# Gateloop attention with a maxout FFN on one core: a new order of all engine lists, a new order of the last output parts, and three unread steps left out of the last group

## The chip, the core and the metric

The kernel runs on one core of a Trainium2 chip. The metric is the device time of one execution in microseconds; a kernel is run several times and the median counts. Beside these runs, one execution is taken with the hardware profiler. Its trace gives the times of every instruction, counted from the start of its span, on TensorE (PE, with its weight loads shown apart as PEld), VectorE (DVE), ScalarE (ACT), GpSimd (POOL) and SyncE (SP, which here only starts DMAs).

## What is computed

All is float32: 4 batches, 8 heads, 768 time steps, head size 48. The first half is a scan with a complex gate, the second a feed-forward layer on its result.

```python
mag = np.sqrt(a_re * a_re + a_im * a_im)
scale = np.minimum(mag, 0.999) / (mag + 1e-06)
a_re_n, a_im_n = (a_re * scale, a_im * scale)
for t in range(S):                       # 768 steps, state D x D per head
    new_re = ar * S_re - ai * S_im
    new_im = ar * S_im + ai * S_re
    kv = np.einsum('bhd,bhe->bhde', k[:, :, t], v[:, :, t])
    S_re, S_im = (new_re + kv, new_im)
    y[:, :, t] = np.einsum('bhd,bhde->bhe', q[:, :, t], S_re)
# x: y as (3072 tokens, 384 features); w1, w2, w3: 384 x 768; w_out: 768 x 384
h = np.maximum(np.maximum(x @ w1, x @ w2), x @ w3)
return h @ w_out
```

## The kernel before

**Groups.** The 768 time steps are cut into 12 groups of 64 (`NG`). In a group, the four batches are two pairs: pair x and pair y, each with its 64 steps of two batches on 128 partitions. A step of the program has a name, the pair where it has one, and its group: `dkx:3` is step `dk` of pair x in group 3.

**The steps of a group.** Loads (`Lr`, `Li` for the gate, `Lk`, `Lq`, `Lv`). The gate's logarithm and angle (`sqr`, `sqi`, `add`, `lnL`, ... `atan`, `turn`), on ACT and DVE. Running sums over time are matmuls with constant matrices: `cs` sums the angles (it needs `turn`), `sums` the logarithms (it needs `Lnop`), `F` makes sums for eighths of a group. `sums` has two halves, one with the matrix `mid` and one with the matrix `rest`. From `mid` come the factors `Ek` and `Eq` on keys and queries, from `rest` comes `En`. Keys and queries are multiplied by cosine and sine (`sa`, `sb`, then `uk`, `uq` on DVE), transposed on PE (`tpk`, `tpq`), copied out of PSUM (`Kc`, `Qc`) and scaled for blocks of time (`Q1`, `Q2`, `QB`, `QG`, `KB` on DVE). `A` and `B` are scores on PE; `g0` to `g3` (DVE) and `b0`, `b1` (ACT) bring them into the lower triangle. For the state that the next group reads, DVE multiplies the keys by `En` (`kEn`), PE multiplies them with the values (`dk`), and `h0` and `h1` add this to the state. `y` is the group's output on PE, from scores, values and state, and `x` copies it to SBUF. The last group has no `dk`.

**The feed-forward part.** In each group after the first, `U01`, `U11`, `U02`, `U12` are the big products with the up weights: 18 matmuls of 128x256 each in the trace. `u01` and `u11` (a maximum with zero) and `u02`, `u12` (a maximum on DVE) read them; the weights `w2` and `w3` are stored as differences from `w1`, whose share reaches the output by the product of `w1` and `w_out`, so two weights in two halves are all that `U` multiplies. The down product is cut into seven block products `P1` to `P7`, with sums of blocks `S1` to `S4` on DVE and two more products `Px`, `Py`. `P1`, `P6` share one half of a PSUM tile, `P5`, `P7` the other; in a second tile `P2`, `P3` write one half, and `P4` writes columns 0 to 191 of the other half, while `Py` has written all its columns. `r1` (ACT), `r6`, `r5`, `r7`, `r57`, `ox`, `oy` and, in the last group, `oz` (all DVE) add the products up into two output tiles, and `Dx`, `Dy`, `Dz` send them out, one DMA from SP's queue and, in the last group, one from ACT's queue. In the last group `oy` and `Dy` have columns 0 to 191 of pair y's output, `oz` and `Dz` columns 192 to 383.

**The first group.** Before group 0 ends, the weights have to be loaded and turned into the form that PE reads. Steps `WL`, `Wa`, `Wb`, `Wc`, `We`, `Wf`, `Wg` do that for twelve parts of the weights, in ACT and DVE between the steps of groups 0 to 2. `T`, `t`, `M`, `m` make the product of `w1` and `w_out` (transposes, their copy on ACT, matmuls, a copy on ACT).

**What sets the order.** The string `SCHEDULE` (lines 21 to 114) lists every step once. `program` runs through it, and each step issues its instructions. `Bound` (line 189) ties each instruction of an engine behind the one before it on that engine, so the list is also the order in which each engine works, and each DMA queue starts. Nothing else moves a step: an engine whose next step has to wait holds all steps behind it. `SLOTS` has a digit for every PSUM tile in the order in which they are asked for: one of four slots of two banks; a tile has to wait until the readers of the tile before it in that slot are done (`banks`, line 208). `OTHER` names the steps that run on their other engine: a copy or an absolute value on DVE in place of ACT, a load started by POOL in place of SP, an addition on DVE in place of a DMA that adds (started by POOL).

All instructions are issued from line 198, so views of the trace are read by tile: `sums<-Ln,rest` is the `rest` half of `sums`, `E<-sums` is `Ek` or `Eq`, `uk<-uk,En` is `kEn`, `cs<-w,upto` is `cs`, `w<-w,ar` is `turn`, `g<-dk` and `g<-g,dk` are `h1`, `vb<-wt` is `t0` or `t1`, `wm<-wo,vb` is `M0` or `M1`, `wm<-wo,uk` is `M2`, `up<-xhx,w` is one of the big products `U`, `op<-...` is one of `P1` to `P7`, `Px`, `Py`, and `ot<-ot,op` is one of `r6` to `oz`.

Of the kernel before, what the change touches and what calls it, by code (L numbers as in the profile page):

```python
# [21 lines left out]
Lix:0 sqi0:0 Zf:0 Zg:0 Lrx:0 xor0:0 sqr0:0 Liy:0 Lry:0 sqi1:0 add0:0 lnL0:0 expe0:0 expw0:0 xor1:0 lne0:0 relu0:0  # L22
Lnop0:0 WL0:0 sqr1:0 Wa0:0 add1:0 CL:0 lnL1:0 expe1:0 Lkx:0 abs0:0 Lix:1 Wb0:0 Wc0:0 We0:0 WL3:0 half0:0 expw1:0 Fx:0
lne1:0 relu1:0 Lnop1:0 pw0:0 Wa3:0 Wf0:0 abs1:0 Wb3:0 half1:0 WL6:0 lnw0:0 expL0:0 f3x:0 Liy:1 f2x:0 Lrx:1 Wc3:0 Wa6:0
f1x:0 Lry:1 mulai0:0 mulw0:0 We3:0 Wb6:0 WL9:0 pw1:0 lnw1:0 stt0:0 expL1:0 mulw1:0 f0x:0 atan0:0 mulai1:0 Wf3:0 T0:0
sqi:1 stt1:0 turn0:0 Wc6:0 atan1:0 Lqy:0 sumsx:0 csx:0 turn1:0 We6:0 Lqx:0 sqr:1 add:1 Wf6:0 Wa9:0 Wb9:0 WL11:0 WL10:0
# [10 lines left out]
b0y:0 Lky:1 b1y:0 kEny:0 Wf7:0 sumsy:1 f3:1 yy:0 mulw:2 xy:0 sb:1 dky:0 u02x:0 stt:2 U02y:0 Lkx:1 h1y:0 Z4:0 mqx:1
atan:2 U11y:0 Lnop:2 Wb8:0 mkx:1 turn:2 sa:1 ukx:1 u11y:0 U01y:0 U12y:0 u01y:0 Eky:1 uqx:1 u02y:0 Eqy:1 cs:2 u12y:0
tpqx:1 Wc8:0 We8:0 mky:1 Eny:1 Lky:2 tpkx:1 Qcx:1 Wf8:0 t:2 Wg7:0 U21y:0 Wg8:0 U21x:0 nfy:2 nfx:2 Q1x:1 Lqx:2 mqy:1
Q2x:1 kEnx:1 uqy:1 u21y:0 U22y:0 u22y:0 u21x:0 af:2 Kcx:1 sumsx:2 F:2 Ax:1 g0x:1 g1x:1 g2x:1 Ekx:2 Enx:2 Eqx:2 Z2:0  # L40
Lvx:1 f1:2 f3:2 KBx:1 h0x:1 uky:1 tpqy:1 f2:2 Qcy:1 Q1y:1 g3x:1 Oy:0 Lvy:2 tpky:1 Q2y:1 mqx:2 Lvy:1 f0:2 Lkx:2 sa:2
sqi:3 oy:0 Lry:3 J3:0 QBx:1 dkx:1 Bx:1 sb:2 h1x:1 U12x:0 QBy:1 uqx:2 QGx:1 U22x:0 Kcy:1 KBy:1 Lrx:3 Lqy:2 u22x:0
u12x:0 Ay:1 b1x:1 g0y:1 g1y:1 g2y:1 g3y:1 b0x:1 mkx:2 sqr:3 tpqx:2 Qcx:2 By:1 yx:1 add:3 lnL:3 QBx:2 expe:3 b0y:1
sumsy:2 xx:1 Eqy:2 Eky:2 expw:3 relu:3 Q1x:2 b1y:1 QGy:1 abs:3 Ox:0 Q2x:2 Lix:4 ukx:2 ox:0 mky:2 mqy:2 Dy:0 uky:2 yy:1
addw:3 tpky:2 lne:3 kEny:1 tpkx:2 Liy:4 Lnop:3 xy:1 xor:3 half:3 Cdy:2 Kcy:2 U11:1 Cdx:2 J1:0 U01:1 Lqx:3 Lrx:4 uqy:2
lnw:3 Kcx:2 KBx:2 J2:0 expL:3 u11:1 Dx:0 Eny:2 mulw:3 mulai:3 stt:3 kEny:2 h0y:1 tpqy:2 atan:3 Lry:4 sqi:4 turn:3
Qcy:2 dky:1 h1y:1 kEnx:2 sumsx:3 u01:1 J4:0 cs:3 Eqx:3 mqx:3 Ax:2 h0y:2 Ekx:3 t:3 sqr:4 add:4 g0x:2 g1x:2 g2x:2 U12:1
Enx:3 Lrx:5 nfx:3 U02:1 lnL:4 expe:4 Q1y:2 nfy:3 expw:4 u12:1 S3:1 af:3 dky:2 g3x:2 relu:4 abs:4 addw:4 Q2y:2 F:3
u02:1 Bx:2 Ay:2 Lvx:2 sb:3 S1:1 f2:3 Lkx:3 h1y:2 f1:3 QGx:2 Lqy:3 P5:1 S2:1 P7:1 f0:3 QBy:2 g0y:2 KBy:2 g1y:2 f3:3
S4:1 lnw:4 g2y:2 P1:1 expL:4 h0x:2 P6:1 r1:1 b0x:2 b1x:2 g3y:2 r6:1 dkx:2 r5:1 r7:1 lne:4 Lry:5 sa:3 Lky:3 r57:1 h1x:2  # L50
sumsy:3 By:2 xor:4 mkx:3 b1y:2 b0y:2 Eny:3 half:4 Cdy:3 Liy:5 yx:2 xx:2 mulw:4 Eky:3 Eqy:3 Py:1 QGy:2 Px:1 P4:1 P3:1
yy:2 ukx:3 uqx:3 xy:2 oy:1 tpkx:3 tpqx:3 mky:3 h0x:3 mulai:4 Kcx:3 Lix:5 sqi:5 stt:4 Qcx:3 Lqx:4 Lky:4 P2:1 uky:3
Lnop:4 atan:4 U01:2 ox:1 u01:2 tpky:3 Lvy:3 QGx:3 Kcy:3 mqy:3 Cdx:3 uqy:3 tpqy:3 turn:4 sumsx:4 Qcy:3 Lrx:6 kEny:3
KBx:3 h0y:3 Lkx:4 Q2y:3 QBx:3 Ekx:4 Enx:4 Q1y:3 Eqx:4 cs:4 F:4 f1:4 mkx:4 t:4 sqr:5 U11:2 u11:2 Lqx:6 f3:4 Q2x:3 f2:4
Dy:1 nfx:4 Q1x:3 nfy:4 Ay:3 add:5 g0y:3 Ax:3 f0:4 g0x:3 g1y:3 g2y:3 af:4 mqx:4 xor:5 Bx:3 g3y:3 sb:4 KBy:3 U02:2 sa:4
g1x:3 U12:2 ukx:4 u02:2 S3:2 g2x:3 tpkx:4 g3x:3 Lvx:3 uqx:4 Lvy:4 lnL:5 expw:5 relu:5 Lqy:4 u12:2 expe:5 Kcx:4 tpqx:4
Qcx:4 dky:3 kEnx:3 dkx:3 S1:2 h1y:3 sumsy:4 S2:2 P5:2 h1x:3 Eqy:4 QBy:3 Dx:1 abs:5 Liy:6 addw:5 b0x:3 b1x:3 lne:5
Lnop:5 half:5 Eky:4 mky:4 Eny:4 mqy:4 Cdx:4 S4:2 Cdy:4 P1:2 P6:2 Py:2 P4:2 r1:2 yx:3 r6:2 r5:2 By:3 lnw:5 expL:5 b0y:3
mulw:5 uqy:4 h0x:4 b1y:3 mulai:5 QGy:3 Px:2 stt:5 atan:5 Lix:6 P3:2 Lry:6 xx:3 sqr:6 Liy:7 P7:2 r7:2 Lkx:5 uky:4 P2:2
tpqy:4 Lky:5 Qcy:4 r57:2 tpky:4 yy:3 sqi:6 ox:2 Lqx:5 kEnx:4 kEny:4 Lvx:4 dkx:4 oy:2 add:6 xy:3 Kcy:4 sumsy:5 turn:5  # L60
sumsx:5 h1x:4 QGx:4 Dy:2 Dx:2 Ekx:5 cs:5 Q1y:4 lnL:6 Lix:7 Eqx:5 U11:3 mkx:5 expw:6 Lvx:5 relu:6 KBx:4 Q2x:4 Enx:5
expe:6 lne:6 h0y:4 Q2y:4 mqx:5 Eky:5 U01:3 Lnop:6 abs:6 Q1x:4 u11:3 t:5 nfy:5 nfx:5 Eny:5 QBx:4 u01:3 Eqy:5 mky:5
xor:6 Ax:4 af:5 g0x:4 addw:6 sb:5 dky:4 h1y:4 sa:5 F:5 half:6 f3:5 uqx:5 g1x:4 g2x:4 lnw:6 expL:6 U12:3 u12:3 f2:5
Lrx:7 f0:5 f1:5 U02:3 tpqx:5 g3x:4 mulai:6 uky:5 tpky:5 Qcx:5 mulw:6 u02:3 Lqy:5 S1:3 Ay:4 Bx:4 S2:3 P1:3 QBy:4 sqi:7
S3:3 mqy:5 b1x:4 P5:3 Kcy:5 b0x:4 KBy:4 g0y:4 P6:3 stt:6 g1y:4 uqy:5 By:4 atan:6 yx:4 ukx:5 P7:3 g2y:4 g3y:4 Lkx:6
Lry:7 sqr:7 QGy:4 b0y:4 b1y:4 Cdy:5 Cdx:5 Q1x:5 tpkx:5 xx:4 Kcx:5 turn:6 tpqy:5 add:7 S4:3 Qcy:5 Lvx:6 r1:3 yy:4 xy:4
sumsx:6 Eqx:6 cs:6 t:6 lnL:7 r6:3 Px:3 kEnx:5 r5:3 Q2x:5 Py:3 P4:3 Enx:6 h0x:5 Ekx:6 xor:7 nfy:6 kEny:5 P2:3 U01:4
r7:3 nfx:6 expw:7 dkx:5 expe:7 lne:7 relu:7 abs:7 r57:3 addw:7 QGx:5 af:6 Lry:8 Lvy:5 h1x:5 mqx:6 sb:6 Lqy:6 u01:4
sumsy:6 QBx:5 sa:6 F:6 Liy:8 U11:4 f3:6 Eqy:6 mkx:6 Q2y:5 Eky:6 KBx:5 mqy:6 P3:3 Lky:6 Q1y:5 f1:6 uqy:6 Lrx:8 h0y:5
f0:6 oy:3 Eny:6 ox:3 Bx:5 u11:4 KBy:5 lnw:7 Ax:5 g0x:5 Ay:5 g1x:5 half:7 g2x:5 expL:7 f2:6 g3x:5 mulai:7 U02:4 g0y:5  # L70
g1y:5 g2y:5 b0x:5 g3y:5 QBy:5 b1x:5 mky:6 yx:5 ukx:6 By:5 Lvy:6 Dx:3 Cdy:6 u02:4 Cdx:6 QGy:5 mulw:7 b1y:5 uqx:6 U12:4
P1:4 S3:4 b0y:5 P7:4 stt:7 atan:7 Lqx:7 xx:5 u12:4 S1:4 tpqx:6 tpkx:6 S2:4 Kcx:6 yy:5 turn:7 Lnop:7 dky:5 Qcx:6 uky:6
Lkx:7 r1:4 sqr:8 sumsx:7 xy:5 h1y:5 cs:7 t:7 kEnx:6 Lix:8 sqi:8 P6:4 Px:4 Py:4 P5:4 P2:4 P4:4 QBx:6 Dy:3 h0x:6 add:8
lnL:8 relu:8 Q1x:6 expw:8 nfx:7 Q2x:6 Eqx:7 expe:8 S4:4 nfy:7 P3:4 tpqy:6 r6:4 KBx:6 Lqx:8 abs:8 Liy:9 r5:4 r7:4 Ekx:7
r57:4 tpky:6 ox:4 oy:4 Enx:7 af:7 dkx:6 Qcy:6 kEny:6 F:7 Dx:4 sa:7 xor:8 h1x:6 half:8 sb:7 h0y:6 Lkx:8 Dy:4 f0:7 f2:7
Q2y:6 f1:7 QGx:6 U11:5 u11:5 Cdx:7 mkx:7 U12:5 Kcy:6 u12:5 Q1y:6 Lry:9 Cdy:7 U01:5 Lrx:9 Lix:9 mqx:7 addw:8 f3:7 ukx:7
# [994 lines left out]
```

## Time and profile before

| | us |
|---|---|
| median of 3 runs | 551.74 |
| lowest and highest run | 549.87, 553.06 |
| the profiled execution, its own time | 552.02 |
| its span, first to last instruction | 550.3 |
| PE busy in the span | 515.6 (94%) |
| DVE busy | 484.8 (88%) |
| ACT busy | 363.8 (66%) |
| POOL busy | 115.6 (21%) |

A row of the table of windows has a stretch of the span, its length, then for PE, PEld, DVE, ACT and POOL the busy time in it with the number of instructions, then PEclk (the mean clock that PE was granted, 1.00 is full), the busy share of the DMA engines and GB/s. A row of waits has the engine and the tile that waited, the engine and tile that ended the wait, the total in us, the number of waits, and the longest. A row of the timeline has start, duration, engine, line, operation, tiles, forms and count, and in brackets the idle time of the engine ahead of it and what ended it; "issue" means that the engine waited for nothing that the profile shows. A row of the chain of work that ended last has start, duration, engine, tile and count. Queue q8 brings PE's instructions.

### The profile page before, as it was taken

The page shows a single profiled execution, that of the slowest core. Times are in us where ns is not written, and L with a number is a line of the kernel's source. Part 1 is how long each engine was busy: PE and PEld are TensorE (multiplying, and loading weights), DVE is VectorE, ACT ScalarE, POOL GpSimd, SP SyncE. Part 2 cuts the span into 40 slices and gives each one's busy share as a digit, 9 for nine tenths or more (in the row PEclk, how much of TensorE's full clock was granted, in tenths as well). Part 3 has the DMA queues.
Part 4 walks back from the last instruction along what each step waited for, and adds up shares of the span by engine and source line. Part 5 has one row for each costly group of instructions (what it writes and reads, how often), then busy time and mean ns, then how long its engine had stood idle before and what let it go on. Part 6 is the DMA issues. An engine that isn't in the chain of part 4 may idle for free.

```text
span 550.3 us, 22368 instructions
## 1 busy us (share of the span) xinstructions
PE 515.6 (94%) x9998; PEld 441.4 (80%) x9998; DVE 484.8 (88%) x735; ACT 363.8 (66%) x568; POOL 115.6 (21%) x167
## 2 busy tenths in 40 slices
PE   2478989999999999999999999999999899999996
PEld 1245578778988888988898988988988788988886
DVE  7999989999999999999999999988999687886325
ACT  6999898688989778696492638677678465221000
POOL 7524180030251222214004001303101250000000
PEclk9769899999999999999999999999999899999999
DMA  8978975553443455244516025356150350010011
GB/s 233 243 206 170 244 129 89 101 92 69 80 89 74 96 111 104 49 91 83 104 42 121 3 52 107 64 105 112 22 104 11 66 117 2 4 30 4 2 29 29
DMA packets 117023, 47.93 MB, mean 87 GB/s; under 512 B 103936, under 2 KB 109536, under 8 KB 116928
## 3 DMA queue, kind: packets, MB, share of 16 engines
q1 hardware_dynamic: 104272, 31.87, 27.4%
q0 software_dynamic: 10304, 14.05, 14.1%
q8 instruction: 78, 1.28, 0.9%
q10 hardware_dynamic: 2352, 0.59, 0.5%
q14 instruction: 17, 0.14, 0.1%
HBM read 33.03 MB, written 4.72 MB: 69 GB/s over the span
## 4 chain that ended last, share of the span: by engine, by line
PE 71%; DVE 10%; issue 2%; ACT 1%; DVEq 0%; ACTq 0%
PE up L198 28%; PE op L198 22%; PE y L198 6%; PE tp L198 4%; PE A L198 3%; PE dk L198 3%; PE sums L198 2%; DVE atm L198 1%; PE B L198 1%; DVE Q L198 1%; PE F L198 1%; DVE QG L198 1%; PE cs L198 1%; DVE uk L198 1%; DVE xhx L198 1%
## 5 line engine op out<-in xcount | busy, mean ns | idle before, releaser
L198 PE MATMUL up<-xhx,w 128*128 128x256 f32 x792 | 177.5, 382 | 0.0
L198 PEld LDWEIGHTS up<-xhx,w 128*128 128x128 f32 x792 | 148.6, 190 | 22.4 <-DVE g L198 2.2
L198 ACT ACT_TABLE_LOAD x50 | 64.2, 1283 | 4.4 <-issue 3.6
L198 POOL DMA_DIRECT2D ar<-nf x44 | 39.9, 1297 | 77.8 <-DVE ar L198 66.7
L198 ACT COPY atm<-B 32x128 f32<-32x128 f32 x96 | 24.5, 256 | 39.4 <-DVE atm L198 24.2
L198 PE MATMUL op<-wo,xhx 128*128 128x192 f32 (+1 forms) x220 | 49.2, 362 | 0.0
L198 DVE TENSOR_TENSOR Q<-Q,f 112x1024 f32<-112x1024 f32 (+1 forms) x48 | 45.3, 951 | 0.4 <-ACT Q L198 0.2
L198 PE MATMUL y<-atm,vb 128*32 128x64 f32 x1152 | 39.4, 221 | 2.9 <-issue 2.9
L198 PEld LDWEIGHTS op<-wo,xhx 128*128 128x128 f32 x220 | 36.7, 190 | 3.3 <-issue 0.6
L198 PEld LDWEIGHTS y<-atm,vb 128*32 128x32 f32 x1152 | 33.1, 110 | 7.3 <-issue 6.2
L198 PE MATMUL y<-QG,g 112*32 112x64 f32 x1408 | 37.3, 220 | 0.5 <-issue 0.5
L198 DVE TENSOR_TENSOR ot<-ot,op 128x192 f32<-128x192 f32 (+1 forms) x67 | 27.1, 413 | 11.0 <-PE op L198 6.2
L198 DVE TENSOR_TENSOR xhx<-xhx,up 128x768 f32<-128x768 f32 x22 | 20.9, 951 | 17.9 <-PE up L198 17.9
L198 PEld LDWEIGHTS y<-QG,g 112*32 112x32 f32 x1408 | 34.6, 110 | 0.7 <-issue 0.7
L198 PE MATMUL op<-wo,strassen 128*128 128x192 f32 x176 | 34.2, 339 | 0.1
L198 POOL DMA_DIRECT2D w<-L x8 | 9.0, 1124 | 117.4 <-ACT L L198 104.8
L198 PE MATMUL op<-w,strassen 128*128 128x192 f32 x176 | 32.8, 329 | 0.0
L198 DVE COPY_PREDICATED atm<-masko,A 128x256 f32<-128x256 uint8 x72 | 31.2, 435 | 1.2
L198 PEld LDWEIGHTS op<-wo,strassen 128*128 128x128 f32 x176 | 30.0, 196 | 2.3 <-issue 0.7
L198 PE MATMUL A<-Q,K 112*32 112x80 f32 x1536 | 30.6, 234 | 0.5 <-issue 0.5
L198 PEld LDWEIGHTS op<-w,strassen 128*128 128x128 f32 x176 | 28.9, 190 | 1.9 <-ACT ot L198 0.8
L198 PEld LDWEIGHTS A<-Q,K 112*32 112x32 f32 x1536 | 27.4, 110 | 3.6 <-issue 1.4
(156 smaller groups left out, 1114.5 us busy)
## 6 DMA issues: line engine op xcount, KB each, us to landing
ai<-in_a_im_dram SPq DMA_DIRECT2D x46, 96.0 KB, 3.4
ar<-in_a_re_dram SPq DMA_DIRECT2D x46, 96.0 KB, 3.3
out_dram<-ot SPq DMA_DIRECT2D x45, 96.0 KB, 3.0
...
```

The costliest lines, as they stand in the source:

```text
L198: ins = f(*a, **kw)
```

## The change

One line of code changes: in the last group `sums` leaves out its `rest` half.

```diff
         if name == "sums":
             ps = T["sums", x] = banks("sums")
-            for n, mat in enumerate((mid, rest)):
+            for n, mat in enumerate((mid, rest) if g < NG - 1 else (mid,)):
```

`SCHEDULE`, `SLOTS` and `OTHER` are replaced as a whole. The new list has the same 1752 steps less four: `Enx:11`, `Eny:11`, `kEnx:11`, `kEny:11`. Of `OTHER`, 32 names go and 37 come: loads of keys, queries and values change between the queues of SP and POOL in both directions; on DVE come `abs:3`, `abs:8`, `af:9`, `u01:8`, `u11:5`, `u11:7`, `Qcy:7`, `Kcx:11`, `Lnop:9` and `addw` of groups 6 to 11; from DVE go `abs:5`, `abs:6`, `af:5`, `af:7`, `af:8`, `u01:3`, `u01:11`, `u11:6`, `addw:5`, and copies `Kc`, `Qc` and `x` of groups 6 to 10, eight of them.

The places of the list that matter most, before and after. The stretch around `cs:1`:

```diff
-uqx:0 tpqx:0 lnw:1 t0:0 Wf11:0 WL1:0 T1:0 WL2:0 Wf10:0 expL:1 Qcx:0 Lky:0 ukx:0 tpkx:0 mulw:1 Wa1:0 t1:0 Cdx:0 Lvx:0
-Eqy:0 Kcx:0 Wa2:0 lne:1 Q2x:0 Fy:0 f2y:0 Wb1:0 f1y:0 WL4:0 kEnx:0 Q1x:0 M0:0 f3y:0 Liy:2 f0y:0 Eny:0 mulai:1 Wb2:0
...
-dkx:0 Lrx:2 Lry:2 sqr:2 add:2 atan:1 lnL:2 Wb4:0 Cdy:0 turn:1 WL5:0 Wg1:0 Wc4:0 M1:0 h1x:0 expe:2 cs:1 relu:2 g1x:0
+Wf1:0 Fy:0 f0y:0 We2:0 stt:1 Wf2:0 Ax:0 Lnop:1 Eky:0 Eqy:0 mqy:0 t0:0 f1y:0 f2y:0 WL4:0 WL5:0 mky:0 f3y:0 g0x:0 sby:0
+sqi:2 sqr:2 add:2 afy:0 dkx:0 h1x:0 M0:0 atan:1 Cdy:0 turn:1 Wa4:0 Wb4:0 M1:0 cs:1 Wg1:0 say:0 M2:0 lnL:2 g1x:0 Wc4:0
```

The stretch from `U12:8` to `yx:9`:

```diff
-KBy:9 Ax:9 g0y:9 lne:11 By:9 U12:8 expw:11 g1y:9 mkx:10 g0x:9 g1x:9 g2y:9 g3y:9 relu:11 P1:8 Lvx:9 b0y:9 abs:11 ukx:10
-g2x:9 g3x:9 S3:8 tpkx:10 u12:8 mqx:10 b1y:9 b1x:9 b0x:9 sumsy:10 F:10 Kcx:10 yx:9 S1:8 f3:10 f1:10 addw:11 Eqy:10 xx:9
+af:10 Ax:9 By:9 expe:11 g2y:9 mkx:10 Eqx:10 U12:8 sa:10 Dy:7 g0x:9 g1x:9 lne:11 expw:11 g3y:9 g2x:9 b0y:9 ukx:10 g3x:9
+b1x:9 tpkx:10 sumsy:10 Lnop:11 b0x:9 u12:8 b1y:9 Dx:7 Kcx:10 F:10 S1:8 f0:10 Lqy:10 f2:10 S3:8 yx:9 kEnx:10 h0x:9 P7:8
+S2:8 abs:11 Eny:10 f1:10 P6:8 P1:8 xor:11 half:11 Cdy:10 addw:11 Eqy:10 mqy:10 uqy:10 Cdx:10 f3:10 QGy:9 P5:8 S4:8
```

The end:

```diff
-u02:11 Dy:10 S3:11 P1:11 r1:11 P2:11 S1:11 S2:11 P5:11 S4:11 P6:11 kEny:11 P3:11 r6:11 r5:11 ox:11 P7:11 P4:11 r7:11
-r57:11 Dx:11 oy:11 Dy:11 oz:11 Dz:11
+P2:10 P3:10 r7:10 r57:10 U01:11 oy:10 Dy:10 u01:11 U02:11 U12:11 ox:10 Dx:10 Py:11 Px:11 u11:11 u12:11 P1:11 r1:11
+u02:11 P2:11 S3:11 S1:11 P5:11 S2:11 S4:11 P6:11 r6:11 P3:11 r5:11 P7:11 ox:11 P4:11 Dx:11 r7:11 r57:11 oz:11 Dz:11
+oy:11 Dy:11
```

More of the change, by code (lines that the diff above doesn't have):

```diff
@@ L21 @@
 SCHEDULE = """
[L22 to L26, printed above, removed]
@@ L37 @@
[L37 to L41, printed above, removed]
@@ L42 @@
[L42 to L76, printed above, removed]
@@ L87 @@
-Lix:11 atan:9 h0x:8 yy:7 Lqy:9 oy:6 tpky:8 xy:7 KBx:8 Cdy:8 Lvx:8 Kcy:8 tpqy:8 sumsy:9 Lkx:9 F:9 Qcy:8 f0:9 U11:7
-sqi:10 ox:6 f2:9 Eqy:9 kEny:8 Eky:9 Cdx:8 Dx:6 turn:9 Q1y:8 u11:7 Dy:6 U12:7 kEnx:8 xor:10 f1:9 dky:7 mqy:9 Eny:9
-sqr:10 add:10 dkx:8 f3:9 mky:9 u12:7 h1x:8 sumsx:9 Q1x:8 Lqx:9 Lry:11 cs:9 Q2y:8 S3:7 lnL:10 Lrx:11 t:9 Liy:11 QGx:8
-Eqx:9 h1y:7 nfx:9 Q2x:8 relu:10 h0y:8 expw:10 U01:7 expe:10 lne:10 abs:10 nfy:9 addw:10 u01:7 U02:7 Ekx:9 half:10
-u02:7 Bx:8 Ax:8 Ay:8 S1:7 sb:9 Enx:9 P5:7 af:9 QBy:8 g0x:8 sa:9 g1x:8 S2:7 g2x:8 g0y:8 P1:7 lnw:10 Lnop:10 KBy:8 g3x:8
@@ new lines @@
+Cdx:5 g0y:4 uqy:5 b1x:4 KBy:4 P5:3 QBy:4 b0x:4 g1y:4 g2y:4 P6:3 sqi:7 Kcy:5 atan:6 yx:4 Lqx:6 Lkx:6 Lry:7 sqr:7 kEny:5
+By:4 g3y:4 P7:3 ukx:5 b1y:4 tpqy:5 QGy:4 b0y:4 QBx:5 Dx:2 turn:6 r1:3 Lry:8 r6:3 tpkx:5 xx:4 r5:3 add:7 Kcx:5 yy:4
+Qcy:5 kEnx:5 xy:4 r7:3 sumsx:6 cs:6 Ekx:6 Q1y:5 xor:7 r57:3 Enx:6 Lqy:6 t:6 nfy:6 nfx:6 lnL:7 expe:7 Py:3 QGx:5 P4:3
+Px:3 af:6 S4:3 lne:7 Eqx:6 expw:7 h0y:5 KBx:5 h0x:5 Q2x:5 sa:6 Lix:8 mqx:6 U01:4 P2:3 u01:4 sb:6 sumsy:6 F:6 dkx:5
+P3:3 h1x:5 Q2y:5 f3:6 relu:7 Eny:6 abs:7 half:7 Eqy:6 mqy:6 f2:6 U11:4 addw:7 oy:3 f0:6 f1:6 ox:3 Ax:5 Lrx:8 mkx:6
@@ new lines @@
+sumsy:7 Lkx:8 Lvx:7 r7:5 r57:5 cs:8 dky:6 kEnx:7 Q1x:7 Lry:10 P3:5 Eky:7 mky:7 Eqy:7 h1y:6 t:8 nfy:8 P4:5 mqy:7 uqy:7
+xor:9 Eny:7 U01:6 expe:9 lne:9 KBx:7 QBx:7 u01:6 U11:6 nfx:8 oy:5 af:8 relu:9 u11:6 h0y:7 Q2x:7 QGx:7 ox:5 uky:7
+tpky:7 Kcy:7 Dy:5 tpqy:7 dkx:7 Qcy:7 sumsx:8 sumsy:8 Ax:7 h1x:7 Ekx:8 Eqx:8 mkx:8 Lqx:8 expw:9 abs:9 U12:6 Eny:8
+kEny:7 Q2y:7 Eqy:8 addw:9 g0x:7 Enx:8 mqx:8 Lvy:8 Q1y:7 g1x:7 g2x:7 g3x:7 U02:6 sa:8 F:8 sb:8 Eky:8 Lky:8 f1:8 u12:6
+uqx:8 tpqx:8 Qcx:8 ukx:8 f0:8 u02:6 S1:6 Bx:7 Lqy:8 Lnop:9 Ay:7 Lvx:8 b1x:7 S3:6 S2:6 g0y:7 half:9 P5:6 Dx:5 mky:8
@@ L119 @@
[L119 removed]
+0123102012312312032102130130103121020120320312303210310130201321032101230102103210321301302132132132
+0110231023131023012300321301102310123223021301302130230200132123102310213023213103203102310321021302
+1301230130120123021013203203121213021302310213023021312103
 """
 OTHER = set("""
[L123 to L124 removed]
```

120 lines of the change are left out of this document (78 added, 42 removed).

## The prediction, made before the change was run

> **What bounds the kernel now.** The page comes first, for its busy times; then the table of windows, cut where PE waited long; then the waits of PE; then the chain that ended last.
>
> ```profile
> PE 515.6 (94%) x9998; PEld 441.4 (80%) x9998; DVE 484.8 (88%) x735; ACT 363.8 (66%) x568; POOL 115.6 (21%) x167
> ```
>
> ```profile
> 10.00:55.70 45.70, 31.35 (x330) 19.12 (x331) 45.19 (x72) 44.89 (x70) 20.51 (x28) 0.81 0.90 221
> 55.70:183.10 127.40, 123.85 (x2588) 102.08 (x2588) 123.41 (x183) 110.16 (x167) 30.14 (x36) 0.99 0.55 102
> 183.10:427.80 244.70, 244.66 (x5188) 216.17 (x5188) 232.24 (x343) 171.99 (x266) 48.23 (x58) 1.00 0.41 79
> 427.80:430.40 2.60, 0.01 (x2) 0.00 (x0) 1.16 (x2) 1.22 (x3) 0.00 (x0) 1.00 0.97 169
> 430.40:434.80 4.40, 4.39 (x100) 4.22 (x101) 2.40 (x3) 2.36 (x5) 0.00 (x0) 0.61 0.24 46
> 430.40:546.20 115.80, 115.73 (x1892) 104.02 (x1892) 76.11 (x115) 30.51 (x56) 9.18 (x12) 0.99 0.12 26
> 546.20:550.30 4.10, 0.00 (x0) 0.00 (x0) 0.62 (x2) 0.00 (x0) 0.00 (x0) 1.00 0.22 48
> ```
>
> The reader is to see four stages. From 10 to 55.7 us DVE is busy 45.19 of 45.70 us and ACT 44.89, while PE waits for them. From 55.7 to 183.1 PE and DVE are both nearly full: DVE leaves 127.40 - 123.41 = 4.0 us, PE 3.6. From 183.1 to 546.2 PE alone decides; it leaves 0.04 us before 427.8 and 0.07 after 430.4, and between them lies one hole of 2.60 us. The last 4.1 us are two additions and the last DMAs. So the time is (DVE's time to 183 us) + (PE's work from there) + (the hole and what it costs) + (the tail).
>
> ```profile
> PE F L198 <- POOL KB L198: 10.8, 1, 10.8
> PE cs L198 <- DVE w L198: 3.7, 1, 3.7
> PE y L198 <- issue: 3.4, 3, 2.6
> PE cs L198 <- ACT g L198: 2.9, 1, 2.9
> ```
>
> The long waits of PE are start-up (10.8, 3.7, 2.9), and one that no engine ended: 2.6 us of "issue" in `y`, which is the hole.
>
> **The steps that nobody reads.** In the stretch where PE decides, one `sums` takes 0.81 us of the chain, and it has as many `rest` as `mid` instructions.
>
> ```profile
> 425.84 0.81 PE sums L198 x16
> L198 PE MATMUL sums<-Ln,rest 64*64 64x192 f32 x192 | 13.2, 331 | 0.0
> L198 DVE TENSOR_TENSOR uk<-uk,En 128x768 f32<-128x768 f32 x24 | 22.8, 952 | 0.2 <-PE tp L198 0.2
> ```
>
> 192 `rest` instructions in 24 `sums` are 8 of each 16, so half of 0.81 goes, twice: about -0.8; another `sums` in the chain took 0.67, so -0.67 is the other end, and I take **-0.7**. The two `kEn` (2 x 0.95 us of DVE) and two `En` on ACT save nothing: after 430.4 DVE is busy 76.11 of 115.80 us, ACT 30.51. They are hidden behind PE.
>
> **The last output part sent sooner: nothing.** The new list puts `oz` ahead of `oy`, both behind `P4`.
>
> ```profile
> 544.70 1.46 PE L198 MATMUL op<-w,xhx 128*128 128x192 f32 x8
> 544.90 0.74 DVE L198 TENSOR_TENSOR ot<-ot,op 128x192 f32<-128x192 f32 x2 [0.74 <-PE op L198]
> 546.21 0.62 DVE L198 TENSOR_TENSOR ot<-ot,op 128x192 f32<-128x192 f32 x2 [0.56 <-PE op L198]
> 546.59 1.10 SPq L198 DMA_DIRECT2D out_dram<-ot  x2
> ```
>
> `r7` and `r57` end at 545.64, `P4` at 546.16, then `oy` and `oz` run, and each queue starts its two DMAs one behind the other. If `oz` could run at 545.65, its DMA would start near 546.05, the other one would start at 546.59 alone, and the second start, about 0.55 us later (half of 1.10), would be gone: -0.55 is that end. But `oz` reads columns of the PSUM half that `P4` writes. `r1:2` shows what that does: it reads only the columns of `P1:2`, which ended at about the time at which this row begins, and stands in the list behind `P6:2`, which writes other columns of the same half.
>
> ```profile
> 188.49 1.46 PE L198 MATMUL op<-w,strassen 128*128 128x192 f32 x8
> 189.99 0.32 ACT L198 COPY ot<-op 128x192 f32<-128x192 f32 x1 [0.77 <-PE op L198]
> ```
>
> ACT stood idle for 0.77 us and started 0.04 us after the end of `P6:2` (188.49 + 1.46). So a reader waits for writes to its half that stand ahead of it, other columns too. `oz` will wait for `P4`, the two additions change places, and so do their DMAs. I take **0**.
>
> **The start and DVE's time to 183 us.** No PE row before `cs:1` at 55.70 changes sides of it; only their order differs. `cs:1` waited for the copy `h1x:0`, although `turn:1` was done at 54.97.
>
> ```profile
> 53.53 0.57 DVE L198 TENSOR_SCALAR xhx<-xhx 128x768 f32<-128x768 f32 x1
> 54.00 0.97 DVE L198 SCALAR_TENSOR_TENSOR w<-w,ar 128x768 f32<-128x768 f32 x1
> 54.87 0.78 ACT L198 COPY g<-dk 112x768 f32<-112x768 f32 x1
> 55.70 1.39 PE L198 MATMUL cs<-w,upto 64*64 64x384 f32 x8 [2.90 <-ACT g L198]
> 57.02 5.27 PE L198 MATMUL wm<-wo,uk 128*128 128x384 f32 x12
> 48.66 4.14 PE L198 MATMUL wm<-wo,vb 128*128 128x384 f32 x12
> 46.98 0.47 ACT L198 ACTIVATE E<-sums 128x384 f32<-128x384 f32 x1
> ```
>
> In the new list `h1x:0` is ahead of `atan:1`, and `Wb4` (0.57) stands behind `turn:1`. So `turn:1` can end at 54.4. Before it PE has `M0` and `M1` (4.14 each), which now come late because the copy `t0` stands behind eleven more ACT steps, the last of them `Eky` and `Eqy`. In the old list `Eky` is the last of these, done at 47.45 with some 1 us of steps ahead of it that the new list puts behind `t0`; so I estimate 46.5. `M0` and `M1` then fill PE to 54.8, with no hole ahead of `cs:1`, so `M2` should take 4.14 in place of 5.27. PE would be some 2 us sooner at 62 us. That alone is no gain, since DVE is full until 183 us. DVE gains only where it waited for PE:
>
> ```profile
> DVE atm L198 <- PE A L198: 1.4, 1, 1.4
> DVE g L198 <- PE dk L198: 0.9, 2, 0.5
> ```
>
> The first is `g0y:0` at 70.8 us, which waited for `A` and so for the late PE: with PE 2 us sooner it goes. In the two `h1` waits (0.9) the new list puts more DVE work ahead of them. DVE's instructions up to 183 us are the same but for `abs:3` and `u01:3`, which about cancel. So the end at one side is -2.3. At the other side new waits of the same kind come in other places, +1.4. I take **-1.0**, near the first wait alone, since steps such as `dkx:3`, at which PE waited for DVE at 183 us, come as late in DVE's new list as in the old.
>
> Loads that change queue, and additions that move from POOL's DMAs to DVE from group 6 on, I cost at nothing: past 183 us DVE has 12 us free before 427.8 and 40 after. If that cover were gone, each moved `addw` would cost 0.95.
>
> **The hole at 427.8 us.** No engine ended it, and the data were there. The queue of PE's own instructions tells why.
>
> ```profile
> q8 instruction: 78, 1.28, 0.9%
> ```
>
> ```profile
> q0 software_dynamic: 121, 0.37, 24.6%
> ```
>
> ```profile
> q0 software_dynamic: 193, 0.45, 95.4%
> q8 instruction: 1, 0.02, 2.1%
> ```
>
> 78 packets bring 1.28 MB, 16.4 KB each, and PE and PEld have 2 x 9998 instructions, 256 to a packet. The first q0 row is all that the DMA engines did from 419 to 427.8 us: no block came in while PE used up what it had. The last two rows are 427.8 to 430.5: one block lands, and PE goes on at 430.41. So this block came late. Counted back from the hole, 22 matmuls of `y`, 64 of `F`, 16 of `sums`, 16 of `tpk` and 8 of `P1:8`, each with its weight load, are 252 instructions, so the block before began about at the end of `U12:8`, at 423.9. If the next is asked for there, it is asked for amid big matmuls, and the small ones behind use up a block in 4 us.
>
> ```profile
> 427.81 2.60 issue
> 430.41 1.94 PE y L198 x91
> 432.36 9.21 PE op L198 x44
> 274.29 7.99 PE op L198 x44
> 441.57 1.72 PE y L198 x112
> ```
>
> Behind the hole the granted clock is 0.61 for 4.4 us: (1 - 0.61) x 4.4 = 1.7. The chain agrees: 44 `op` take 9.21 against 7.99, and 91 `y` take 1.94 where 1.72 x 91/112 is 1.40: 1.22 + 0.54 = 1.76. The hole costs 2.6 + 1.7 = 4.3 us. If the block is in time in the new order, **-4.3**; if it comes late again, 0, or +1.3, since `P1:8` (1.3 us), which covered a part, now stands behind `y`. I take -4.3, because of 78 blocks one came so late, and what stands before and behind most block ends differs now.
>
> The Trainium skill, page "Runtime: NRT & Kernel Launch", section "Instruction fetch mechanics", says that an engine's instructions come in 16 KiB blocks of 256, the next fetched while the current one runs, and that the cost of crossing a block is mostly hidden. The size agrees with 16.4 KB; "mostly hidden" does not hold at 427.8. By it no order would gain here, and the sum would be 550.3, as in the first rival below. The Trainium skill, page "TensorE: Matmul & The Clock Gate", section "Part 1: The HAM clock gate", lets the clock fall after an idle window of about 3.4 us; here 2.60 us were enough for 0.61. By it the term would be -2.6 and the sum 547.7, the fourth rival.
>
> **The sum**, against the profiled execution's own 552.02 (span 550.3 and 1.7 around it; the runs' median is 551.74, 0.3 less): 552.0 - 0.7 - 0 - 1.0 - 4.3 = **546.0 us**.
>
> **The rivals.** *The late block comes again.* For: PE has as many instructions ahead of `U12:8` in both lists, so the same block ends there; and `tpk`, `sums`, `F` and `y` follow at once. Or the hole has a cause that no order touches. Against: a shift by a few instructions, such as waits of PE's own, puts the ask among small matmuls. Time: 552.0 - 0.7 - 1.0 = 550.3, with 1.3 more 551.6. This is no change.
>
> *Slower: two late blocks.* Each block end in a big matmul with a run of small ones behind it can make a hole; without `P1:8` ahead of `y` one costs 2.6 + 1.3 + 1.7 = 5.6 us. With none the time is 546.0, with one 551.6, with two 557.2. From two on the change is slower.
>
> *DVE's waits only move.* The first hundred microseconds are new in many places, and PE's gain to 62 us is eaten by waits on DVE. Then the -1.0 is 0 or +1.4: 547.0 to 548.4, still faster if the hole goes.
>
> *The hole goes, the clock still falls* for a reason of its own: the row of 0.61 then stays, 546.0 + 1.7 = 547.7. The chain, where the slow rows follow the hole at once, speaks against it.
>
> *The tail does shorten*, if `oz` need not wait: 545.5.
>
> **How the numbers follow.** Forecast (546.0, own range 544 to 548) 0.40; the late block again (550.3 to 551.6) 0.32; two late blocks (557.2) 0.14; waits moved (547.0 to 548.4) 0.08; the clock's fall stays (547.7) 0.03; shorter tail (545.5) 0.03. A measurement of this kernel can tell about 0.5% from no change, 2.8 us: faster is below 549.0, slower above 554.5. Forecast, moved waits, clock and tail are faster, 0.54; the late block is the same, 0.32; two are slower, 0.14. The range reaches from 544.0 (the forecast with -2.3 and a shorter tail is 544.2) to 552.5, one late block with 0.9 for moved waits; above it lies the case of two late blocks.
>
> **What would show it.** In the new profile: no "issue" row above 1 us after 180 us and no clock below 0.9 there, against a hole in `y` of group 9 near 424 us. `M2` at 4.1 us and no wait above 1 us ahead of `cs:1`. `g0y:0` without a wait. The last two additions directly behind `P4`, and about 4.1 us from PE's end to the span's end. `sums` of group 11 with 8 instructions. The prediction is wrong if DVE is idle for more than 4 us between 55 and 183 us, or if PE has a second hole.

## The result, and the profile after

The new kernel takes **553.47 us** (median of 12 runs, 551.23 to 554.33), the old one 551.41 on the same chip (12 runs, 548.69 to 553.06). The ratio is 1.004, with a 95% interval from 1.0022 to 1.0057: slower by 1.2 to 3.1 us. The forecast was 546.0, and its range ended at 552.5. The profiled execution of the new kernel took 553.04 us, 1.0 more than that of the old one.

First the table of windows of the new kernel, cut at its own hole near 430 us.

```profile
55.70:183.10 127.40, 122.51 (x2559) 100.77 (x2558) 122.58 (x181) 108.39 (x166) 33.42 (x43) 1.00 0.56 108
...
183.10:429.50 246.40, 245.11 (x5197) 216.37 (x5195) 231.90 (x340) 172.96 (x269) 46.23 (x58) 1.00 0.32 64
429.50:431.50 2.00, 0.59 (x27) 0.38 (x25) 2.00 (x4) 1.95 (x5) 0.00 (x0) 1.00 0.74 134
431.50:436.00 4.50, 4.50 (x109) 4.41 (x109) 4.36 (x7) 4.37 (x8) 2.08 (x4) 1.00 0.03 5
```

The reader is to see two things. Around 430 us PE still has a hole, but PE is granted its full clock behind it (1.00 where it was 0.61). And the two stages that were nearly full have lost time: PE leaves 4.9 us before 183 us (3.6 before the change) and 1.3 from there to 429.5 (0.04 before). The waits of PE from 62.3 us on name them.

```profile
PE B L198 <- issue: 1.8, 1, 1.8
PE y L198 <- issue: 1.6, 3, 1.0
PE op L198 <- DVE g L198: 1.1, 1, 1.1
```

These are three holes, in the timeline of PE at 149.6, 276.9 and 430.5 us:

```profile
151.40 0.22 PE L198 MATMUL B<-QB,KB 112*32 112x32 f32 x1 [1.79 <-issue]
...
278.04 0.43 PE L198 MATMUL op<-wo,strassen 128*128 128x192 f32 x1 [1.12 <-DVE g L198]
...
429.93 0.32 PE L198 MATMUL y<-atm,vb 128*32 128x64 f32 x8 [0.38 <-ACT atm L198]
431.49 0.22 PE L198 MATMUL y<-atm,vb 128*32 128x64 f32 x1 [1.03 <-issue]
```

The second is put down to DVE, but it is a late block too. If the rows of PE and PEld, those that only wait for a semaphore included, are numbered in order of time, 1.79, 1.12 and 1.03 end at rows 4545, 10177 and 16321; each of these leaves 193 when divided by 256, and so does the row at which the hole of the old kernel ended (16321). In all 13 profiles of this study, PE has 55 idle times of 0.5 us or more between 60 us and the tail. 46 of them end at a row of this kind, 2.2 to 3.2 us (median 2.4) after a packet of PE's instruction queue began to move. The other nine are plain waits for ACT or DVE. So a hole is called an idle time **at a block end** below if it ends at such a row.

The start went as the prediction's small steps said, but without the gain. In the timeline of PE there is no hole ahead of `cs:1`, and `M2` takes 4.14; in that of DVE `g0y:0` (70.35) does not wait.

```profile
48.48 8.92 PE L198 MATMUL wm<-wo,vb 128*128 128x384 f32 x24
57.33 0.88 PE L198 MATMUL cs<-w,upto 64*64 64x384 f32 x8
58.14 4.14 PE L198 MATMUL wm<-wo,uk 128*128 128x384 f32 x12
```

`M2` ends at 62.28 us; in the old kernel it ended at 57.02 + 5.27 = 62.29. Nothing was gained up to here. At that point PE has done the same steps in both kernels, so the rest can be compared from there. The table gives, for every profile (one execution each), PE's time from the end of `M2` to the end of `P4:11`, split by the rows of the trace into busy time, idle time at block ends (above 0.2 us each) and other idle time, and the tail from PE's end to the span's end. The labels are explained with the experiments.

| us | M2's end | PE from there | busy | block ends | other idle | tail |
|---|---|---|---|---|---|---|
| old list: before | 62.3 | 483.9 | 477.7 | 3.6 | 2.6 | 4.15 |
| e3, a whole block more | 64.9 | 483.4 | 476.4 | 4.1 | 2.8 | 4.14 |
| e2, half a block more | 62.0 | 505.4 | 485.6 | 16.9 | 2.9 | 4.15 |
| e1, last group's edits | 61.6 | 485.8 | 476.5 | 6.4 | 2.9 | 4.15 |
| e5, the same, rows back | 60.5 | 484.3 | 476.8 | 4.7 | 2.9 | 4.16 |
| e6, addw:11 on DVE | 60.7 | 485.1 | 477.6 | 4.3 | 3.2 | 4.15 |
| e9, three edits | 61.3 | 481.8 | 476.6 | 2.2 | 3.0 | 4.15 |
| e10, the same, 8 rows more | 61.0 | 485.4 | 478.1 | 3.9 | 3.3 | 4.15 |
| new list: after | 62.3 | 484.5 | 476.8 | 4.4 | 3.2 | 4.51 |
| e4, a whole block more | 66.1 | 485.8 | 476.9 | 5.3 | 3.6 | 4.51 |
| e7, addw:4 on DVE | 61.3 | 487.1 | 476.9 | 2.4 | 7.8 | 4.51 |
| e8, work in a wait | 61.8 | 486.3 | 476.9 | 4.1 | 5.3 | 4.52 |
| e11, 8 rows more | 60.4 | 486.8 | 478.2 | 4.3 | 4.3 | 4.52 |

The busy time holds what the low clock costs: by windows of 3 us, 1.7 in before, 1.5 in e6, 1.4 in e10 and 4.5 in e2, and nothing in the other rows. Without it the old list has 476.0 to 476.8 but for e2 (481.1), and the new one 476.8 to 476.9 in four profiles and 478.2 in the fifth.

### The profile page after: what moved, and what is told of

Read it like the earlier page. It is cut to its first block, busy times and chain, and to the rows that moved or that the text cites. A ratio compares the mean times of both kernels' runs of the same rounds, so it can differ in the third digit from the quotient of the medians.

```text
span 551.3 us, 22338 instructions
## 1 busy us (share of the span) xinstructions
PE 514.5 (93%) x9982; PEld 441.6 (80%) x9982; DVE 482.6 (88%) x730; ACT 368.7 (67%) x575; POOL 120.6 (22%) x177
## 4 chain that ended last, share of the span: by engine, by line
PE 65%; ACT 11%; DVE 7%; issue 2%; DMA 1%; DVEq 0%; ACTq 0%
PE up L198 25%; PE op L198 21%; PE y L198 6%; PE A L198 3%; ACT L198 3%; PE tp L198 3%; PE dk L198 2%; PE sums L198 2%; ACT CS L198 1%; DVE g L198 1%; PE B L198 1%; ACT f L198 1%; ACT L L198 1%; PE F L198 1%; DVE w L198 1%
## 5 line engine op out<-in xcount | busy, mean ns | idle before, releaser
L198 POOL DMA_DIRECT2D ar<-nf x44 | 42.1, 1308 | 96.8 <-DVE ar L198 95.6
L198 POOL DMA_DIRECT2D k<-in_k_dram x32 | 28.2, 1051 | 62.2 <-DVE uk L198 55.6
L198 ACT ACTIVATE xhx<-up 128x768 f32<-128x768 f32 x18 | 14.6, 812 | 34.6 <-PE up L198 34.5
L198 PEld LDWEIGHTS op<-wo,strassen 128*128 128x128 f32 x176 | 28.8, 190 | 2.8 <-DVE g L198 1.8
```

Source lines behind the costliest of these rows:

```text
L198: ins = f(*a, **kw)
```

## The experiments

**Theory.** The holes come from where the 256-instruction blocks end in PE's work, and from what stands in the DMA queues when the next one is asked for. The new list made one shorter and brought others. **Rival.** The holes are waits on work and data of their own place, and the new list is slower by its waits on DVE and ACT.

**Runs e2, e3 and e4: only the block ends move.** Tiny matmuls are put ahead of the first `F`, where PE waits some 11 us anyway; 32 in e2, 64 in e3 and e4.

```diff
         T["F", g * C + c] = fs[g % 2][:, c]
+        for _ in range(32 if T["word"] == "Fx:0" else 0):
+            mm(out=ps[0:3, 0, 0:3], lhsT=biases[:, 0:3], rhs=biases[:, 0:3], start=True, stop=True)
         for i in range(2):
```

> The old list, with 32 tiny matmuls (3 columns, 64 instructions of PE) ahead of the first F, where PE waits 10.8 us anyway; nothing else differs, but every 256-instruction block now ends 64 instructions earlier in the work. Theory (holes belong to block ends): the hole in y of group 9 near 427.8 us changes size or goes, and holes can come at other block ends; without any the time falls by 4.3 to about 547, each new one gives back 1 to 4. Rival (the hole belongs to the work or the data at that place): it stays 2.6 us at 427.8, and the time is that of before within 0.5.

> As the one with 32, but 64 tiny matmuls: block ends 128 instructions earlier in the work. Theory (holes belong to block ends): again other holes than at a shift of 0 and of 64, and a time between 546 and 553 by their sum. Rival (the hole belongs to the work): 2.6 us at 427.8 as before, and the same time.

> The new list with 64 tiny matmuls ahead of the first F: block ends 128 instructions earlier. In the new list as it is, PE has holes of 1.79 us at 149.6 (B of group 2), 1.12 at 276.9 (P5 of group 4) and 1.03 + 0.38 at 430 (y of group 9). Theory (holes belong to block ends): these three go or change size, others can come; without any the time falls by 4.3 from 553.5 to about 549. Rival (they are waits on DVE and on data that the new order brought): all three stay where they are, and the time is 553.5 within 0.5.

The pages of e2 and e3 show that the counts of instructions in these expectations were wrong by a factor of two:

```profile
PE 522.6 (91%) x10062; PEld 446.7 (78%) x10062; DVE 486.6 (85%) x735; ACT 364.0 (64%) x568; POOL 115.8 (20%) x167
```

```profile
PE 515.9 (93%) x10126; PEld 442.6 (80%) x10126; DVE 484.9 (88%) x735; ACT 363.9 (66%) x568; POOL 114.1 (21%) x167
```

32 matmuls added 64 matmul rows and 64 weight loads to the 9998 of each, 128 instructions: half a block. 64 added a whole block, which leaves every block end where it was in the work. That made a control of e3 and e4.

Measured: e2 **573.0 us**, ratio 1.036 (1.0319 to 1.0401), 21.6 us more than before, with the same work in the same order. e3 555.89 (ratio 1.0067, 1.0036 to 1.0099), e4 558.03. In e3 and e4, `M2` ends 2.6 and 3.8 us later than without the added block, which is most of what they lost; behind it e3 has the hole of before, at the same matmul and of the same length, and e4 those of the new list (1.80 at `B`, 1.39 at `P5`, 1.30 at `y`) and one of 0.78 at 122.2. In e2 the waits of PE from 62.3 us on are these:

```profile
PE y L198 <- issue: 7.2, 5, 3.1
PE dk L198 <- issue: 3.2, 4, 1.2
PE F L198 <- issue: 2.6, 4, 1.6
PE sums L198 <- issue: 2.0, 1, 2.0
PE A L198 <- issue: 1.9, 2, 1.2
```

What follows: a hole belongs to a block end and not to the work at that place, which settles it for the theory. In the old list the place of the ends is worth some 20 us, and this list has them in a good place: a whole block keeps it, half a block does not. For the new list half a block was not run. Against before's profile, e2's is 21.2 us longer: 13.3 in idle time at block ends, 2.8 in low clock and 5.1 in longer busy time of the same steps, which is not traced.

**Runs e1 and e5: the last group's edits alone, and with the rows put back.** e1 is the old list with the diff of `sums`, without `En` and `kEn` of group 11, and with `oz Dz` ahead of `oy Dy`. e5 differs in this:

```diff
+                        if n == 1 and g == NG - 1:
+                            mm(out=ps[0:3, ch, HC:HC + 3], lhsT=biases[:, 0:3], rhs=biases[:, 0:3], start=True, stop=True)
+                            continue
```

> The old list with the edits of the last group alone: sums of group 11 without the rest half, no En and kEn of group 11, oz and Dz ahead of oy and Dy. By the prediction's terms: 0.7 us less than before (16 matmuls of sums, 0.67 to 0.8) and nothing from the tail, so about 550.7. A rival: the tail does shorten by 0.55, so 1.2 us less. PE's instruction stream is the old one up to sums of group 11, so if the place of a block's end in the list makes the late block, the hole in y of group 9 near 427.8 us must be there again, 2 to 3 us long, with the low clock behind it; if the hole is chance from execution to execution it is gone or somewhere else.

> As the run with the last group's edits alone, but each of the four matmuls of the rest half in sums of group 11 is replaced by one of 3 columns whose result nobody reads, so that PE's instruction count, and with it the place of every block's end, is that of the old list. Theory (taking 32 instructions out moved the later block ends, which made the new holes of 1.32 us at dky of group 10 and 0.83 us at A of group 11): both holes go, the hole of y of group 9 stays, and the time is that of before less 0.5, about 551. Rival (the new tail order or the missing En and kEn cost the 1.5 us): the time stays at 553.

Measured: e1 553.0 us, ratio 1.0026 (1.0003 to 1.005): **slower** than before, with work taken away. e5 551.55, ratio 1.0013 (0.9986 to 1.0041). The timeline of PE in e1 has two holes that before does not have:

```profile
454.12 0.37 PE L197 MATMUL dk<-vb,uk 64*48 64x48 f32 x11 [1.32 <-issue]
...
502.51 0.28 PE L197 MATMUL A<-Q,K 112*32 112x80 f32 x4 [0.83 <-issue]
```

They are at block ends (rows 17345 and 19137). In e5 PE does not wait from 440 to 545 us. So taking out 32 instructions moved the later block ends by 16 and 32 rows, and that cost 2.15 us of holes where 0.7 was to be won. That the holes come and go is shown, by one profile each; the difference of the two times (1.45 by the medians) is not, since their intervals overlap. The hole at `y` of group 9 is there in both (2.3 us), so it is no chance of one execution.

**Run e6: does the late block wait behind a burst?**

```diff
-xy:11 u01:11 u11:11
+xy:11 u01:11 u11:11 addw:11
```

> The old list with one step on another engine: the addition addw of group 11 is done by DVE and not by POOL's accumulating DMA, whose 3072-byte packets fill all 16 DMA engines from 425.5 to 427.9 us, just ahead of the late block's packet at 427.97. Theory (the block waits behind that burst): the packet comes some 2 us sooner, the hole at y of group 9 falls from 2.6 us to 1.4 or less, as in the new list, where this addition is on DVE as well, and the low clock behind it goes: 3 to 4 us less, 547.5 to 548.5. Rival (asking amid big matmuls is late by itself): the hole stays above 2 us and the time within 0.7 of before. The 0.95 us that DVE gets should cost nothing or up to 0.95.

The view of the DMAs of the old kernel from 425.5 to 427.95 us, just ahead of the late packet at 427.97, has one queue and no instruction block:

```profile
q0 software_dynamic: 125, 0.38, 92.0%
...
w<-L POOLq DMA_DIRECT2D x1, 384.0 KB, 6.0
```

The second row is an issue shortly before, at 424.4: `addw:11`, which POOL starts as a DMA that adds. Measured: e6 **548.70 us**, ratio 0.9966 (0.9947 to 0.9984), 1 to 3 us less than before. The packet of that block starts 3.1 us after its block end was reached, where it was 4.8 (before), 4.7 (e1, e5) and 4.8 (e3), and the hole is

```profile
431.48 0.25 PE L198 MATMUL y<-atm,vb 128*32 128x64 f32 x2 [0.68 <-issue]
```

with no low clock behind it. The median of e6 shows the gain, its profile does not: this execution took 551.6 us, where ten of the twelve runs took 547.9 to 549.5, and it has a hole of 3.11 at `F` (67.1 us) with 1.5 us of low clock behind it.

That the block was late because it waited behind the burst is not shown. In e6 another burst (`Ln<-e`) moves ahead of the packet; this is queue q0 from 424.2 to 429.2 us:

```profile
q0 software_dynamic: 144, 0.39, 43.2%
```

The new list has `addw:11` on DVE too. Its packet starts 3.4 us late (after), 4.2 (e4) and 4.8 (e11); ahead of the first no other packet moves, ahead of the others one burst for the last 0.5 and 0.3 us. And the blocks that begin at 115.4 us in e4 and at 109.7 in e11 have their packets 4.6 us late with no other packet moving in between. So a block can come as late as the one at 427.8 without any burst, and how much of its 4.8 us the burst made is open.

**Run e7: the same at the new list's hole at 149.6.** `addw:4` is added to `OTHER`.

> The new list with the addition addw of group 4 done by DVE and not by POOL's accumulating DMA, which is the first of two such bursts that fill the DMA engines from 144 to 148.9 us, ahead of the block's packet at 149.05. Theory (the block waits behind the bursts): the packet comes some 2 us sooner and the hole of 1.79 us at B of group 2 (149.6) goes; DVE, which is full until 183 us, gets 0.95 us more, so 0.8 to 1.8 us less than the new list, about 552. Rival (the ask itself is late, amid the big matmuls of P): the hole stays, and the time is that of the new list or up to 0.95 more.

Measured: 554.93 us, ratio 1.0078 (1.0057 to 1.0099), 1.5 more than the new list by the medians. The burst goes and the hole goes, as expected; the packet is 2.6 us late where it was 4.6 (after), 4.6 (e4), 4.7 (e8) and 4.8 (e11), each of these behind bursts. Here the two go together, in one profile. But the time does not fall. The addition now stands in DVE's queue behind `g<-g,dk` until 151.56, and the three waits that follow are those of ACT, of DVE and of PE:

```profile
ACT L L198 <- DVE w L198: 2.7, 1, 2.7
```

```profile
DVE uq L198 <- ACT CS L198: 2.3, 1, 2.3
```

```profile
PE tp L198 <- DVE uk L198: 2.1, 1, 2.1
PE tp L198 <- DVE uq L198: 1.8, 1, 1.8
PE y L198 <- ACT atm L198: 0.9, 1, 0.9
```

ACT waits for the addition, the cosine comes late, `uq:3` waits for it, and PE waits 0.9 + 1.8 near 155 us in place of the 1.79 at 149.6. The first row of PE (2.1) is at 61.3 us, and comes up again below. So what cures the hole past 423 us, where DVE has room, does not where DVE and ACT are full.

**Run e8: the clock at the start.** 16 tiny matmuls ahead of `F`, and 48 ahead of the transposes of `tpqx:0`, in PE's wait of 2.88 us:

```diff
+            raw = banks("tp")
+            for _ in range(48 if T["word"] == "tpqx:0" else 0):
+                mm(out=raw[0:32, 0, 0:64], lhsT=ident[:, 0:32], rhs=ident[:, 0:64], start=True, stop=True)
```

> The new list with 64 idle matmuls, 256 instructions, a whole block, so that block ends stay where they were in the work: 16 tiny ones ahead of the first F and 48 of 32x64 in PE's wait of 2.88 us ahead of tpq of group 0 (34.3 to 37.2 us). In the new list PE then runs at half its clock from 36.5 to 50.4 us, which made sums, A, dk and M0 3.5 us longer than in the old one. Theory (the wait makes the clock fall, and that is why M0 came late and the start gained nothing): the clock stays at full from 37 us on, M0 takes 4.14 in place of 5.05 and M2 ends about 3 us sooner than 62.3; what of it reaches the end is at most what DVE waits for PE before 183 us, 0 to 2 us. Rival (the clock falls for another reason): half clock as before, and nothing gained.

The window from 36.5 to 50.4 us, first of the new kernel, then of e8:

```profile
36.50:50.40 13.90, 11.86 (x217) 9.70 (x218) 13.72 (x19) 13.78 (x22) 5.89 (x7) 0.51 0.70 148
```

```profile
36.50:50.40 13.90, 12.28 (x311) 10.65 (x309) 11.23 (x16) 11.35 (x19) 4.23 (x6) 1.00 0.72 145
```

The clock stays full, and `M0` and `M1` take 8.01 in place of 8.92. But the idle matmuls took longer than the wait that they were to fill: `tpqx:0` ended at 42.2 in place of 38.3, and DVE stood still for 2.1 us behind it. The time is 555.97 (ratio 1.0099, 1.0079 to 1.012). So the price of the low clock cannot be read from the time. The timeline of PE tells something else:

```profile
57.71 4.14 PE L198 MATMUL wm<-wo,uk 128*128 128x384 f32 x12
63.90 0.27 PE L198 MATMUL tp<-ident,uk 64*112 64x64 f32 x2 [2.06 <-DVE uk L198]
```

With `M2` done at 61.84, PE waits 2.06 us for `uk` from DVE; in e7, where the clock was 0.72 from 40 to 50 us by chance and `M2` ended at 61.25, it waits 2.1 at the same place. DVE was late in both, by what they added or by their own start. The new kernel's own DVE has this `uk` at

```profile
61.19 0.95 DVE L198 TENSOR_TENSOR uk<-CS,k 128x768 f32<-128x768 f32 x1
```

It ends at 62.14, and `M2` at 62.28. The next step of PE, `tpky:0`, reads it, so an `M2` done sooner would have helped PE there by 0.14 us and no more.

**Run e9: the edits that the runs point to, on the old list**, that is e5 with `addw:11` on DVE, and with the last additions in the old order (`oy Dy` ahead of `oz Dz`; the expectation below says the new one).

> Three edits that the runs point to, together on the old list: addw of group 11 on DVE (2.6 us less by itself), the rest half of sums of group 11 replaced by four matmuls of 3 columns so that block ends stay, and En and kEn of group 11 left out; the tail in the new order. If the terms add: 548.7 of the run with addw alone, less about 0.5, so 548.2, faster than both kernels. If sums of group 11 was covered after all: 548.7.

Measured: **549.51 us**, ratio 0.9959 (0.9937 to 0.9982), the fastest by ratio with e6, from which it cannot be told apart. It is above the 548.2 expected if the terms add, so that they add is not shown. Both beat both kernels. Its waits at block ends:

```profile
PE y L197 <- issue: 1.5, 3, 1.0
PE F L197 <- issue: 0.8, 1, 0.8
```

**Runs e10 and e11: 8 rows more**, two tiny matmuls ahead of `F`, on e9 and on the new list.

> The same, with 2 tiny matmuls (8 instructions) ahead of the first F, so that block ends fall 8 instructions earlier in the work. Counted on the trace of the old list, the time by which 256 instructions run in less than 3.25 us (0.8 for the ask and 2.45 for the load) sums to 9.5 us over all blocks as they lie and to 5.1 with a shift of 8, against 21 with a shift of 128, which cost 21. If this count decides, the time falls, by at most 4 us; if the late asks decide, which it leaves out, it can go either way by 1 to 3 us, with holes at other rows.

> The new list with the same 2 tiny matmuls. The same count is 6.4 us as its blocks lie and 7.3 with a shift of 8. Theory (holes decide): the holes at 149.6, 276.9 and 430.5 change size, and the time moves by 1 to 3 us, rather up. Rival (waits on other engines made the new list slower, not its holes): the time stays at 553.5 within 0.5, whatever the holes do.

Measured: e10 550.72 (ratio 0.9992, 0.9968 to 1.0016), e11 554.29 (1.0058, 1.0036 to 1.0081). The count of short blocks did not decide: e10 has holes of 1.8, 0.6 and 1.05 us where e9 has 0.8, 0 and 0.95. In e11 the hole at 276.9 is down to 0.21, which shows that it was not a wait for DVE, the one at 149.6 is 1.46, and a new one of 1.31 comes at 156.7. Holes change places with 8 rows; the sum stays (4.3 against 4.4). e11's time is within 1 us of the new list, so it does not tell the rival's share from the theory's.

## Why the prediction was wrong, point by point

**The hole, -4.3: the step that failed.** At its own place the step was half right: the hole fell from 2.60 to 1.03 us and the low clock behind it went. But the step says "I take -4.3, because of 78 blocks one came so late, and what stands before and behind most block ends differs now". The second half of that sentence speaks against the first. An old list in which one end of 78 is bad is a good one (half a block away it loses 21.6 us), and new ends are new chances for holes. Idle time at block ends went from 3.6 to 4.4 us, so the term is +0.8 in idle time, and -0.9 with the low clock that before's profile had (1.7). Profiles of the old list whose blocks end at the same places have 3.6, 4.1 and 4.7 (before, e3, e5), so the 0.8 is within the spread; what is clear is that the 2.6 were not won. The rival of two late blocks had the mechanism right for two of the three holes, where the block ahead began in the big matmuls of `op` and `up` (ahead of the one at 276.9 it began in `y`); its price of 5.6 for each was too high, since none of the new holes drew a low clock and none was longer than 1.8.

**Why this block was late** stays open. The prediction saw that q0 filled the DMA engines, read only that no block came in, and put it down to an ask amid big matmuls; the runs neither show nor refute that, and do not settle what the burst ahead of the packet did. In the part on DVE's time it costs the additions that move from POOL's DMAs to DVE at nothing; e6 shows that one of these, `addw:11`, was worth 1 to 3 us by itself, and e7 that another one costs where DVE and ACT are full.

**The low clock, 1.7 of the 4.3,** was taken as fixed. It is not: before has 0.61 behind a hole of 2.60, e3 has 1.00 behind the same hole of 2.60, e1 and e5 have 1.00 behind 2.32. Before's profile was an unlucky one here. Over the whole span, 23 of 72 later executions of the old kernel have a mean clock as low as this one's 0.978 or lower; where it fell in them is not on record.

**DVE's time to 183 us, -1.0: came out at nothing or worse.** Its parts came true (`M2` at 4.14, no wait ahead of `cs:1`, `g0y:0` without a wait, `t0` done at 46.3 against the estimate of 46.5). The sum did not: `M2` ended when it had ended before, and even an earlier `M2` would have found DVE's `uk` not done before 62.14 us, a wait that the step did not look for. The clock fell to 0.51 from 36.5 to 50.4 us (0.88 in the old profile), and `sums`, `A`, `dk` and `M0` ran long; the step had `M0` start at about 46.5, and it started at 48.48. Then DVE lost time: it leaves 127.40 - 122.58 = 4.8 us from 55.7 to 183.1 where it left 4.0, which is the sign that the prediction had named for being wrong. 0.99 of it is `nfy:1`, which waits for ACT's `t:1`. The largest part stands behind the hole of PE at 149.6:

```profile
153.28 1.22 DVE L198 TENSOR_TENSOR QG<-Q,f 112x1024 f32<-112x1024 f32 x1 [1.59 <-PE y L198]
```

**sums, -0.7: the right size, but not free.** The group went from 192 to 176 `rest` instructions and from 13.2 to 12.0 us of busy time, but these overlap with their neighbours. From the start of `sums` to the start of the next step, PE took 0.86 and 0.70 us in the old kernel's last group and takes 0.54 and 0.35 in the new one's, so the term is 0.67. e1 shows what it brings with it.

**The tail, 0: right for the order, not for the kernel.** Two additions stand directly behind `P4`:

```profile
545.28 1.46 PE L198 MATMUL op<-w,xhx 128*128 128x192 f32 x8
545.48 0.74 DVE L198 TENSOR_TENSOR ot<-ot,op 128x192 f32<-128x192 f32 x2 [0.74 <-PE op L198]
546.78 0.62 DVE L198 TENSOR_TENSOR ot<-ot,op 128x192 f32<-128x192 f32 x2 [0.56 <-PE op L198]
```

The tail is 4.15 in all eight profiles of the old list (within 0.01), two of them (e1 and e5) with the new order of the last steps, so the order is worth nothing, as forecast. All five of the new list have 4.51. Their DMAs start at the same distance from PE's end, and the last one lands 3.19 us behind it in the new kernel, 3.18 in the old. The 0.36 us come after that: SP, which then only waits for semaphores, has 0.37 us between two of its rows where it had 0.06. In all five profiles of the new list, and in none of the old, a packet of another instruction queue (q14) starts 4.2 us behind PE's end. That SP meets the end of an instruction block of its own there would fit, but is not shown.

**What the prediction left out: time lost between the holes.** Other idle time is 2.6 to 3.3 us in the profiles of the old list, e2 among them, and 3.2 to 4.3 in those of the new one, beside e7 and e8 (7.8 and 5.3), which hold waits that their own additions made. Busy time without low clock is 0.8 us longer in the new kernel's profile than in before's, although 0.7 of `sums` is gone; profiles of the old list differ by as much among themselves. No single step changed by more than 0.3 us apart from those named, so this is not traced to a place. The chain of work that ended last shows the kind. From 180 to 240 us, in the old kernel, then in the new:

```profile
by line: PE op L198 31.1%; PE up L198 26.6%; PE y L198 11.3%; PE dk L198 6.8%; PE tp L198 5.2%; PE sums L198 4.8%; PE A L198 4.1%; PE cs L198 2.1%; PE B L198 1.6%; DVE xhx L198 1.5%; DVE uq L198 1.4%; DVE atm L198 1.3%; PE F L198 1.2%; DVE 
```

```profile
by line: PE op L198 18.0%; PE y L198 8.7%; ACT L198 6.4%; ACT L L198 5.3%; DMA vb<-in_v_dram 4.7%; ACT f L198 3.7%; issue 3.2%; DVE atm L198 3.2%; ACT xhx L198 3.2%; DVE strassen L198 3.2%; DVE w L198 3.0%; PE dk L198 2.9%; DVE Q L198 2.9%;
```

In the old list PE alone decides there; in the new one the chain goes through ACT, DVE and a load of values, so a late step of any of these can delay the end; by how much is not measured. The prediction's "From 183.1 to 546.2 PE alone decides" was read from the old list and carried to the new one.

**The sum.** From profile to profile: low clock -1.7, idle at block ends +0.8, other idle +0.6, `sums` -0.7, tail +0.4, busy time not traced +1.5, together +0.9, as the spans (550.32 and 551.25) differ. Without the low clock in before's profile it is +2.6, and the medians differ by 2.06. So what holes do is shown, and the term of the hole is 3.4 of the 7.0 us by which the forecast missed the profiled execution. The greater part of the loss against the old kernel lies outside the holes and is not traced: it is spread over many small waits and steps.
